# Three fp32r products for the scores of whole key chunks, and accumulating DMAs for a third of the softmax sums

## The chip, the cores and the metric

The kernel runs on one core of a Trainium2 chip. The metric is device time in microseconds (us): the median of separate runs of the whole program. One execution was also taken with the hardware profiler; all rows below come from it.

## What is computed

Soft-capped attention for 4 batches of 12 heads with 448 positions and 64 channels a head, and behind it a mixer over tokens and one over channels, each with a residual path. Cut to what matters:

```python
scores = scale * np.matmul(q, k.transpose(0, 1, 3, 2))
scores = cap * np.tanh(scores / cap)
attn = np.exp(scores - max)
attn = attn / (np.sum(attn, axis=-1, keepdims=True) + 1e-09)
x = np.matmul(attn, v)                     # heads side by side: 4 x 448 x 768
h = np.maximum(x^T @ w_tok1, 0.0) @ w_tok2
u = x + h^T
out = u + np.maximum(u @ w_ch1, 0.0) @ w_ch2
```

## The kernel before

Heads are worked in pairs: 24 pairs `(b, p)`, six a batch. A pair's queries and keys lie in one tile `qkraw` of 128 partitions, one head in partitions 0 to 63 and the other in 64 to 127, queries in `raw[:, 0]` and keys in `raw[:, 1]`. The 448 keys are cut into chunks: three whole ones of 128 and a rest of 64. A *unit* `(b, p, c)` is one chunk of a pair (`c` 0 to 2), or the rest of two neighbouring pairs packed together (`c == NF`), so that two pairs make seven units, and the kernel has 84.

For a unit TensorE forms the scores (`qk_unit`, L176), keys as weights and queries streamed, once for each head `j`, into two PSUM banks; a whole chunk takes two f32 matmuls at L182, one with the weights in the upper 64 rows of the array and one in the lower 64, and an f32 matmul runs as two instructions. ScalarE applies tanh into a tile `e` (L195; eight buffers for all units) and then exp in place (L200). TensorE multiplies by the values (L217, packed L226) and `evac` (L279, VectorE) empties that bank.

The sums over the keys that the softmax divides by are collected by `add_up` (L232). For chunk 1 VectorE adds chunks 0 and 1 into `acc` (L239), for chunk 2 it adds that chunk (L245), and `add_packed` adds the rest in two operations of 64 partitions (L257). An `e` buffer is free once its add is done. Two pairs share one `acc` tile; when both are done, `add_rows` (L259) sums over the partitions with matmuls against ones (L265), and `gather`, `norm`, `spread` and `scale_pair` follow one step apart: copies and small DMAs on SP's queue (`sums`, `rs`, `rb`), a reciprocal, and the multiply that writes `u` (L303). Only then can a pair be transposed (L326) for the token mixer.

Everything up to the end of the attention is in an order written out by hand: 42 steps of two units. In one step each engine gets, in this order, the multiplications by the values for the step's two units, the scores, tanh and exp of the units two steps ahead, the due evacuations, `add_up`, then `background` work, and last what was put off by `at(d, f, 2)` (`scale_pair` and the decoding of weights among it). `at(d, f, y)` runs `f` in place `y` of the step `d` later. `background` feeds TensorE with the token mixer of the batch before (L326, L353, L373), a budget of one ninth of a batch's work in every step. A tile's next load is issued once the last score that reads it has been issued: `load_pair` (L159) for the pair three further on, on SP's queue.

The weights come as 64-bit numbers and are decoded by VectorE, ScalarE and GpSimd (L99 to L119); GpSimd does one subtraction a piece (L119) and nothing else of weight. The token and channel mixers already use three products of high and low parts in fp32r (L353, L373, L552, L569); fp32r is a 4-byte type that TensorE multiplies in one instruction. The channel mixer begins at about 210 us and is not touched.

Of the kernel before, what the change touches and what calls it, by code (L numbers as in the profile page):

```python
# [9 lines left out]
F32R = mybir.dt.float32r  # L10
I32 = mybir.dt.int32
AF = mybir.ActivationFunctionType
ALU = mybir.AluOpType
PSUM = bass.MemoryType.PSUM

P = 128
B, H, S, D = 4, 12, 448, 64
# [6 lines left out]
NF = NK - 1  # L24
# [9 lines left out]
FREE = 40.0  # L34
EPS = 1e-9
WARM = 2


@with_exitstack
def tile_softcap_mixer(ctx, tc, qk, v, cap, w1, w2, wc1, wc2, out):  # L40
    nc = tc.nc
# [30 lines left out]
    def at(d, f, y=0):  # L72
        later.setdefault((now[0] + d, y), []).append(f)
# [76 lines left out]
    pi = in_att.enter_context(tc.tile_pool(name="pi", bufs=2))  # L150
# [3 lines left out]
    def half(i, j):  # L154
        return slice((i ^ j) * D, ((i ^ j) + 1) * D)

    raws = {}

    def load_pair(b, p):  # L159
        raw = pi.tile([P, 2, S], F32, tag="qkraw", name="qkraw", bufs=3)  # L160
        if b == 0 and p == 0:
            nc.sync.dma_start(raw[:, 0], qk[b, p, :, 0])
            nc.scalar.dma_start(raw[:, 1, :P], qk[b, p, :, 1, :P])
            nc.sync.dma_start(cap_sb, cap)
            nc.sync.dma_start(raw[:, 1, P:], qk[b, p, :, 1, P:])
        else:
            nc.sync.dma_start(raw, qk[b, p])
        raws[b, p] = raw

    def load_v(b, p):  # L170
        nc.sync.dma_start(vn[p % 3], v[b, p])

    scores = {}
    es = {}

    def qk_unit(b, p, c):  # L176
        ps = ps_a.tile([P, 2, 512], F32, tag="a", name="ps_qk")
        if c < NF:
            raw = raws[b, p]
            for j in range(2):  # L180
                r = slice(j * D, (j + 1) * D)
                nc.tensor.matmul(ps[:, j, :S], raw[r, 1, c * P:(c + 1) * P], raw[r, 0], start=True, stop=True)  # L182
        else:
            for i in range(2):
                raw = raws[b, p + i]
                for j in range(2):
                    r = slice(j * D, (j + 1) * D)
                    nc.tensor.matmul(  # L188
                        ps[half(i, j), i, :S], raw[r, 1, NF * P:S], raw[r, 0], start=True, stop=True
                    )  # L190
        scores[b, p, c] = ps
# [6 lines left out]
    def exp_unit(b, p, c):  # L198
        e = es[b, p, c]
        nc.scalar.activation(e, e, AF.Exp, scale=near)  # L200
# [29 lines left out]
    accs = {}  # L230

    def add_up(b, p, c):  # L232
        q, i = divmod(p, 2)
        if c == 0:
            return
        if c == 1:
            if i == 0:
                accs[b, q] = pe.tile([P, 2, 2, S], F32, tag="acc", name="acc", bufs=2)
            nc.vector.tensor_tensor(accs[b, q][:, i], es.pop((b, p, 0)), es.pop((b, p, 1)), op=ALU.add)  # L239
            if i == 1:  # L240
                add_packed(b, p)
                es.pop((b, p - 1, NF))
        elif c == 2:
            t = accs[b, q][:, i]
            nc.vector.tensor_tensor(t, t, es.pop((b, p, 2)), op=ALU.add)  # L245
            if i == 1:
                left[b] += 1
                at(1, lambda: work.insert(0, (add_rows(b, q), lambda: True)))
        else:
            add_packed(b, p)  # L250

    def add_packed(b, p):
        q, i = divmod(p, 2)
        for j in range(2):
            r = half(i, j)
            t = accs[b, q][r, i, j]
            nc.vector.tensor_tensor(t, t, es[b, p - i, NF][r, i], op=ALU.add)  # L257

    def add_rows(b, q):  # L259
        ps = ps_c.tile([P, 512], F32, tag="c", name="ps_s")  # L260
        acc = accs.pop((b, q))
        for i in range(2):
            for j in range(2):
                r = (2 * i + j) * SP
                nc.tensor.matmul(ps[r:r + SP, :S], ones, acc[:, i, j], start=True, stop=True, tile_position=(0, r))  # L265
        yield 750, True

        def take():
            x = px.tile([P, S], F32, tag="xs", name="xs", bufs=1)
            nc.vector.tensor_copy(x, ps[:, :S])  # L270
            at(pace[0], lambda: gather(b, q, x))

        read_at(b, None, take)
# [126 lines left out]
    work = []  # L400
# [56 lines left out]
    zeros = nc.const_aps.tensor(0.0, [P, HALF], F32)  # L457
    for _ in range(WARM):
        nc.tensor.matmul(idle[:, :HALF], zeros[:, :P], zeros, start=True, stop=True)
# [16 lines left out]
    def scores_of(t):  # L476
        two = units[2 * t:2 * t + 2]
        for unit in two:
            qk_unit(*unit)
        for unit in two:  # L480
            tanh_unit(*unit)
        for unit in two:
            exp_unit(*unit)
        for i in range(len(two)):
            for n, pair in enumerate(pairs):
                if last_score[pair] == 2 * t + i:
                    raws.pop(pair)
                    if n + 3 < len(pairs):
                        load_pair(*pairs[n + 3])

    scores_of(0)
    scores_of(1)
    for t in range(steps_in):
        two = units[2 * t:2 * t + 2]
# [10 lines left out]
        for b, p, c in two:  # L505
            add_up(b, p, c)
            n = pairs.index((b, p))
# [244 lines left out]
```

## Time and profile before

| | us |
|---|---|
| median of 3 runs | 606.57 (606.2 to 607.16) |
| the profiled execution | 605.01 |
| its span | 603.0 |
| TensorE busy in the span | 592.0 |
| VectorE busy | 384.9 |
| ScalarE busy | 254.5 |
| GpSimd busy | 54.5 |

The busy time is the union of an engine's instructions. A matmul's end is modelled, so that consecutive matmuls overlap in the records: the pace of a stream is read from its starts, or from a run of many. The chain of work that ended last follows the profile back from its end, at each step to what released the next piece. Times inside the program are counted from the span's start.

### The profile page before, as it was taken

How to read it: one execution, taken by the hardware profiler on the slowest of the kernel's cores; microseconds unless marked ns; L12 is line 12 of the kernel's file. 1: busy time of each engine (PE TensorE's matmuls, PEld its weight loads, DVE VectorE, ACT ScalarE, POOL GpSimd, SP SyncE). 2: the span in 40 equal slices, each digit the busy share in tenths (PEclk: the TensorE clock that was granted, in tenths of full speed). 3: DMA queues.
4: the chain of work that ended last, by engine and by line, in shares of the span. 5: the costliest groups of instructions: out<-in, count | busy, mean ns of one | idle time of the engine just before them, and what ended most of it. 6: DMA issues, size and time to landing. Idle time of an engine off the chain costs nothing.

```text
span 603.0 us, 7760 instructions
## 1 busy us (share of the span) xinstructions
PE 592.0 (98%) x3012; PEld 438.2 (73%) x3012; DVE 384.9 (64%) x626; ACT 254.5 (42%) x330; POOL 54.5 (9%) x48
## 2 busy tenths in 40 slices
PE   8998999999999999999999999999999999999997
PEld 2232444444444589997999999999989999999986
DVE  2899879696996996547788386438643853333324
ACT  7998987888878733114332122012211220000000
POOL 0021000000010000002331022001200120000000
PEclk9999999999999999999999999999999999999999
DMA  6545434244442201001343121202120200000224
GB/s 202 170 127 160 148 123 152 78 158 144 135 156 81 68 31 32 0 1 36 104 124 123 34 70 59 83 0 76 66 70 1 70 1 1 1 1 0 93 100 180
DMA packets 24620, 49.12 MB, mean 81 GB/s; under 512 B 6784, under 2 KB 16512, under 8 KB 24576
## 3 DMA queue, kind: packets, MB, share of 16 engines
q1 hardware_dynamic: 24288, 48.37, 24.9%
q8 instruction: 25, 0.41, 0.3%
q14 instruction: 19, 0.16, 0.1%
q10 hardware_dynamic: 288, 0.18, 0.1%
HBM read 42.86 MB, written 5.59 MB: 80 GB/s over the span
## 4 chain that ended last, share of the span: by engine, by line
PE 89%; DVE 5%; ACT 3%; issue 1%; DMA 1%; POOL 0%; SPq 0%; DVEq 0%
PE ps_g L552 29%; PE ps_o L569 29%; PE ps_pv L217 8%; PE ps_qk L182 8%; PE ps_h L353 5%; PE ps_u L373 5%; PE ps_s L265 2%; PE ps_pv L226 2%; PE ps_qk L188 1%; PE ps_t L326 1%; ACT e L195 1%; DVE acc L257 1%; ACT e L200 1%; DVE acc L239 1%; DMA qkraw<-in_qk 1%
## 5 line engine op out<-in xcount | busy, mean ns | idle before, releaser
L569 PE MATMUL ps_o<-g,wc 128*128 128x448 f32 x864 | 182.7, 367 | 0.0
L569 PEld LDWEIGHTS ps_o<-g,wc 128*128 128x128 f32 x864 | 161.6, 188 | 15.2 <-DVE u L574 0.9
L552 PE MATMUL ps_g<-uhl,wc 128*128 128x448 f32 x648 | 138.4, 367 | 0.0
L552 PEld LDWEIGHTS ps_g<-uhl,wc 128*128 128x128 f32 x648 | 120.9, 188 | 10.3
L574 DVE TENSOR_TENSOR u<-u,ps_o 128x448 f32<-128x448 f32 (+1 forms) x145 | 86.7, 612 | 46.8 <-PE ps_o L569 46.6
L195 ACT ACTIVATE e<-ps_qk,tsc 128x896 f32<-128x896 f32 x84 | 81.1, 1022 | 27.9 <-PE ps_qk L182 25.5
L200 ACT ACTIVATE e<-e,near 128x896 f32<-128x896 f32 x84 | 83.5, 1057 | 0.0
L119 POOL TENSOR_TENSOR wc<-wz,wc 128x512 fp32r<-128x512 f32 x36 | 48.2, 1341 | 385.4 <-ACT wc L118 361.9
L557 ACT ACTIVATE g<-ps_g 128x896 fp32r<-128x896 f32 x24 | 22.0, 916 | 142.5 <-PE ps_g L552 142.5
L558 DVE SCALAR_TENSOR_TENSOR g<-ps_g,g 128x896 fp32r<-128x896 f32 x24 | 26.1, 1088 | 75.1 <-ACT g L557 75.1
L182 PE MATMUL ps_qk<-qkraw 64*128 64x448 f32 x288 | 66.1, 570 | 1.0 <-DMA qkraw<-in_qk 0.9
L217 PE MATMUL ps_pv<-e,vn 128*64 128x448 f32 x288 | 64.2, 556 | 0.5 <-ACT e L195 0.5
L182 PEld LDWEIGHTS ps_qk<-qkraw 64*128 64x128 f32 x288 | 24.0, 186 | 42.9 <-issue 12.1
L118 ACT ACTIVATE wc<-wz 128x512 fp32r<-128x512 f32 x36 | 22.7, 629 | 74.6 <-PE ps_g L552 33.9
L552 PE MATMUL ps_g<-last_u,wc 128*128 128x448 f32 x216 | 45.6, 367 | 0.4 <-PE ps_o L569 0.3
L552 PEld LDWEIGHTS ps_g<-last_u,wc 128*128 128x128 f32 x216 | 40.4, 188 | 4.7 <-issue 0.7
L104 ACT ACTIVATE wz<-wraw 128x512 f32<-128x512 f32 x36 | 24.2, 673 | 46.1 <-DMA wraw<-in_wc 27.9
L217 PEld LDWEIGHTS ps_pv<-e,vn 128*64 128x64 f32 x288 | 16.5, 135 | 33.4 <-issue 15.9
L107 DVE TENSOR_SCALAR wz<-wz 128x512 f32<-128x512 f32 (+1 forms) x40 | 17.4, 435 | 34.8 <-ACT wz L104 34.7
L353 PEld LDWEIGHTS ps_h<-wc,last_u 128*128 128x128 f32 x176 | 30.4, 188 | 8.0 <-issue 6.0
L353 PE MATMUL ps_h<-wc,last_u 128*128 128x384 f32 x176 | 36.0, 343 | 0.0
L373 PE MATMUL ps_u<-last_u,wc 128*128 128x448 f32 x144 | 34.1, 375 | 1.5 <-DVE wc L362 0.8
(50 smaller groups left out, 414.3 us busy)
## 6 DMA issues: line engine op xcount, KB each, us to landing
wraw<-in_wc SPq DMA_DIRECT2D x36, 512.0 KB, 3.6
qkraw<-in_qk SPq DMA_DIRECT2D x23, 448.0 KB, 3.3
vn<-in_v SPq DMA_DIRECT2D x24, 224.0 KB, 3.4
rb<-rs SPq DMA_DIRECT2D x48, 112.0 KB, 2.8
out_t<-u SPq DMA_DIRECT2D x23, 224.0 KB, 1.9
wraw<-in_w SPq DMA_DIRECT2D x2, 512.0 KB, 4.7
wraw<-in_w SPq DMA_DIRECT2D x2, 448.0 KB, 3.7
sums<-xs SPq DMA_DIRECT2D x48, 1.8 KB, 2.3
```

The source lines that it names most:

```text
L104: nc.scalar.activation(zf, bits(r[:, :, 1]), AF.Abs, scale=2.0 ** -16)
L119: nc.gpsimd.tensor_tensor(lo, zf, hi, op=ALU.subtract)
L182: nc.tensor.matmul(ps[:, j, :S], raw[r, 1, c * P:(c + 1) * P], raw[r, 0], start=True, stop=True)
L195: nc.scalar.activation(e, scores.pop((b, p, c))[:, :, :S], AF.Tanh, scale=tsc)
L200: nc.scalar.activation(e, e, AF.Exp, scale=near)
L217: nc.tensor.matmul(ps[j * D:(j + 1) * D, :S], vn[p % 3][:, j * NF + c], es[b, p, c][:, j], start=first, stop=last)
L353: nc.tensor.matmul(ps[:, :HALF], w, x, start=(n == 0), stop=(n == len(mm) - 1))
L373: nc.tensor.matmul(ps[:, :S], h1[:, hi, t, cs], w2s[:, wi, t, :], start=(n == 0), stop=(n == 3 * NT - 1))
L552: nc.tensor.matmul(ps[:, i, :S], w[:, wi, cc, fs], uhl[b][:, ui, cc, :], start=(n == 0), stop=(n == 3 * NC - 1))
L558: nc.vector.scalar_tensor_tensor(g[:, 1], ps[:, :, :S], 0.0, g[:, 0], op0=ALU.max, op1=ALU.subtract)
L569: nc.tensor.matmul(ps[:, :S], w[:, wi, i, cs], g[:, gi, i, :], start=(n == 0), stop=(n == 3 * GF - 1))
L574: nc.vector.tensor_tensor(u[b][:, cc, r], u[b][:, cc, r], ps[:, r], op=ALU.add)
```

## The change

In batches 1 to 3 the scores of the whole chunks are formed from a high and a low part. For each pair there `load_pair` also issues, on GpSimd's queue, a DMA that reads the first 832 columns of the pair (448 of the queries, 384 of the keys) from memory a second time and casts them to fp32r (`hi`); two steps later VectorE subtracts it from `qkraw` into `lo`. `qk_unit` then issues three fp32r matmuls for each head (high by high, low by high, high by low) in place of one in f32, head by head within a term. The packed rest still reads `qkraw` in f32, and batch 0 is as before.

In batches 1 and 2 and in the first two thirds of batch 3 the add of chunk 2 (L245) is taken from VectorE: a DMA on GpSimd's queue adds the `e` tile into `acc`. For the first pair of two it is issued behind the packed add, one unit later than the add before; `add_rows` comes one step later. The region that GpSimd's DMA descriptors are kept in is cut to 4096 bytes a partition.

```diff
+SPLIT = S + NF * P
+TERMS = ((0, 0), (1, 0), (0, 1))
...
     def load_pair(b, p):
...
         raws[b, p] = raw
+        if b:
+            hi, lo = (pi.tile([P, SPLIT], F32R, tag=f"qk{x}", name=f"qk{x}", bufs=3) for x in ("hi", "lo"))
+            nc.gpsimd.dma_start(hi, qk[b, p].rearrange("p x s -> p (x s)")[:, :SPLIT])
+            rest = raw.rearrange("p x s -> p (x s)")[:, :SPLIT]
+            at(2, lambda: nc.vector.tensor_tensor(lo, rest, hi, op=ALU.subtract), 2)
+            parts[b, p] = hi, lo
...
     def qk_unit(b, p, c):
         ps = ps_a.tile([P, 2, 512], F32, tag="a", name="ps_qk")
-        if c < NF:
+        if c < NF and b:
+            two = parts[b, p]
+            ks = slice(S + c * P, S + (c + 1) * P)
+            for n, (x, y) in enumerate(TERMS):
+                for j in range(2):
+                    r = slice(j * D, (j + 1) * D)
+                    nc.tensor.matmul(ps[:, j, :S], two[x][r, ks], two[y][r, :S], start=(n == 0), stop=(n == 2))
+        elif c < NF:
...
     def add_up(b, p, c):
         q, i = divmod(p, 2)
+        by_dma = 0 < b < B - 1 or b == B - 1 and q < H // 4 - 1
...
         elif c == 2:
-            t = accs[b, q][:, i]
-            nc.vector.tensor_tensor(t, t, es.pop((b, p, 2)), op=ALU.add)
+            if not by_dma:
+                t = accs[b, q][:, i]
+                nc.vector.tensor_tensor(t, t, es.pop((b, p, 2)), op=ALU.add)
+            elif i == 1:
+                add_third(b, p)
             if i == 1:
                 left[b] += 1
-                at(1, lambda: work.insert(0, (add_rows(b, q), lambda: True)))
+                at(2 if by_dma else 1, lambda: work.insert(0, (add_rows(b, q), lambda: True)))
         else:
             add_packed(b, p)
+            if by_dma:
+                add_third(b, p)
+
+    def add_third(b, p):
+        q, i = divmod(p, 2)
+        nc.gpsimd.dma_start(accs[b, q][:, i], es.pop((b, p, 2)), accum_op=ALU.add)
...
-    nc = bacc.Bacc("TRN2", target_bir_lowering=False, num_devices=1)
+    nc = bacc.Bacc("TRN2", target_bir_lowering=False, num_devices=1, dynamic_dma_scratch_size=4096)
```

## Rows read from the trace of the kernel before

**Rows 1.** The page: engines' busy time, and TensorE's granted clock in 40 slices.

```profile
PE 592.0 (98%) x3012; PEld 438.2 (73%) x3012; DVE 384.9 (64%) x626; ACT 254.5 (42%) x330; POOL 54.5 (9%) x48
PEclk9999999999999999999999999999999999999999
```

**Rows 2.** Busy time by stretch: length, PE, PEld, DVE, ACT, POOL, clock, DMA, GB/s.

```profile
31.00:52.30 21.30, 19.01 (x104) 5.53 (x101) 20.76 (x33) 21.30 (x24) 3.88 (x4) 1.00 0.47 142
52.30:64.00 11.70, 11.67 (x68) 4.25 (x72) 11.48 (x20) 9.52 (x12) 1.13 (x1) 1.00 0.30 102
64.00:85.00 21.00, 21.00 (x122) 9.64 (x114) 16.78 (x28) 18.15 (x23) 0.00 (x0) 1.00 0.41 129
85.00:209.00 124.00, 122.13 (x664) 56.53 (x664) 101.43 (x167) 102.09 (x127) 7.98 (x6) 1.00 0.41 128
```

**Rows 3.** Waits of TensorE, 20 to 90 us: total us, times, longest.

```profile
PE ps_t L326 <- DVE u L303: 1.9, 1, 1.9
```

**Rows 4.** Longest wait of TensorE and of ScalarE, 64 to 209 us.

```profile
PE ps_t L326 <- DVE wc L340: 0.9, 2, 0.7
ACT e L195 <- PE ps_qk L182: 20.2, 14, 2.0
```

**Rows 5.** The chain that ended last, 30 to 82 us: start, us, what.

```profile
51.57 0.62 DVE u L303
...
52.33 1.10 PE ps_t L326 x8
...
66.96 1.70 PE ps_qk L182 x8
```

**Rows 6.** TensorE in order of time, two units' scores at 201 us: start, us.

```profile
201.13 0.65 PE L182 MATMUL ps_qk<-qkraw 64*128 64x448 f32 x2
...
201.99 0.92 PE L182 MATMUL ps_qk<-qkraw 64*128 64x448 f32 x4
202.37 0.54 PE L182 MATMUL ps_qk<-qkraw 64*128 64x448 f32 x2
202.84 0.47 PE L373 MATMUL ps_u<-last_u,wc 128*128 128x448 f32 x1
```

**Rows 7.** The chain that ended last, channel mixer: 36 fp32r matmuls.

```profile
296.84 7.36 PE ps_g L552 x36
```

**Rows 8.** VectorE's groups by shape up to 340 us: busy us, mean ns.

```profile
L245 DVE TENSOR_TENSOR acc<-acc,e 128x896 f32<-128x896 f32 x24 | 26.1, 1087 | 2.7 <-ACT e L200 2.0
L439 DVE TENSOR_TENSOR uhl<-u,uhl 128x448 fp32r<-128x448 f32 x18 | 10.4, 617 | 0.9 <-ACT uhl L438 0.6
L108 DVE TENSOR_SCALAR wz<-wz 128x512 int32<-128x512 int32 x22 | 10.8, 497 | 0.5
L108 DVE TENSOR_SCALAR wz<-wz 128x448 int32<-128x448 int32 x2 | 2.6, 1276 | 0.1
```

**Rows 9.** In order of time, single stretches of GpSimd, VectorE and ScalarE.

```profile
50.19 1.21 POOL L119 TENSOR_TENSOR last_u<-wz,last_u 128x448 fp32r<-128x448 f32 x1 [8.06 <-DVE last_u L116]
50.45 1.20 DVE L108 TENSOR_SCALAR wz<-wz 128x448 int32<-128x448 int32 x1
60.31 1.75 DVE L257 TENSOR_TENSOR acc<-acc,e 64x448 f32<-64x448 f32 x2
64.16 1.90 ACT L195 ACTIVATE e<-ps_qk,tsc 128x896 f32<-128x896 f32 x2
94.54 1.25 DVE L257 TENSOR_TENSOR acc<-acc,e 64x448 f32<-64x448 f32 x2
98.87 1.97 ACT L195 ACTIVATE e<-ps_qk,tsc 128x896 f32<-128x896 f32 x2 [1.60 <-PE ps_qk L182]
```

**Rows 10.** DMA issues: count, KB each, median us from issue to landing.

```profile
qkraw<-in_qk SPq DMA_DIRECT2D x23, 448.0 KB, 3.3
rb<-rs SPq DMA_DIRECT2D x48, 112.0 KB, 2.8
sums<-xs SPq DMA_DIRECT2D x48, 1.8 KB, 2.3
```

More of the change, by code (lines that the diff above doesn't have):

```diff
@@ L157, in tile_softcap_mixer @@
     raws = {}
+    parts = {}
     def load_pair(b, p):
@@ L487, in scores_of @@
                     raws.pop(pair)
+                    parts.pop(pair, None)
                     if n + 3 < len(pairs):
```

## The prediction

> **What bounds the kernel now.** I read the page first. TensorE is busy 98% of the span, at the upper of its two clock levels (2.4 GHz) in every slice [rows 1], so no time is to be had from the clock. An engine that full doesn't show where another sets the pace, so I read the busy times by stretch next. Up to about 52 us ScalarE is never idle (21.30 of 21.30) and VectorE nearly so (20.76), while TensorE has gaps; from 52.3 to 64 us VectorE is still full (11.48 of 11.70); from 64 us on TensorE is full and the other two have about a fifth of their time free [rows 2]. The waits say it more sharply. Before 64 us TensorE stands once for long, 1.9 us at a transpose that waits for VectorE's scaling [rows 3]; the chain that ended last runs over VectorE to that multiply and goes to TensorE with the transpose [rows 5]. From 64 to 209 us TensorE's longest wait is 0.9 us in all, and it is ScalarE that waits for TensorE's scores, 20.2 us [rows 4]. So a shorter score in batches 1 to 3 (they begin at about 45 us) is worth its full length from 64 us on, and work added to VectorE before 64 us is paid in full.
>
> **The scores: from 0.375 to 0.204 us a slot, but three slots for two.** Eight f32 instructions make two units. They start in twos, one for each half of the array's rows: 201.13, 201.99, 202.37 (with a start between the first two of these, left out), and the next work begins at 202.84 [rows 6]. So a unit is two slots of 0.375 us (202.37 less 201.99, rounded), and 1.71 - 4 x 0.375 = 0.21 us go to entering and leaving this tiling once for two units; that stays. After the change a unit is three slots of one fp32r pass. No row has such a pass with the array split. The nearest is the channel mixer's on the whole array, of the same 448 columns: 7.36 / 36 = 0.204 us [rows 7], weight load hidden. I take it. The gain is 54 units x (2 x 0.375 - 3 x 0.204) = 54 x 0.138 = 7.5 us. Bounds while the halves still run side by side: half an f32 slot, 0.1875 us, gives 10.1 us; a slot longer than the whole array's by a tenth, 0.224, for two weight loads and two banks at once, gives 4.2 us.
>
> **VectorE: 18 subtractions in, 16 adds out.** A subtraction has 832 elements a partition. Between 617 ns for 448 elements and 1087 ns for 896 [rows 8] that is 617 + 470 x 384 / 448 = 1020 ns, 18.4 us in all; the adds of chunk 2 that go are 16 x 1.087 = 17.4 us. In sum nothing, but not in place. The first pair of batch 1 is loaded in step 4, the next in steps 6, 8, 10 and 11, so that the subtractions stand in steps 6, 8, 10, 12 and 13. Two of them come before the scaling at 51.57 us, where VectorE is full, and the first add that goes is at step 11. VectorE's idle time in that stretch is 21.30 - 20.76 = 0.54 us [rows 2]. So the transpose at 52.33 us comes 2 x 1.02 - 0.54 = 1.5 us later, more if the idle bits can't be used: 1.8 us. Bounds: 0.5 (ScalarE, full as well, hides some) and 3.5 us (the third subtraction counts too, against one add). Behind 64 us VectorE has a fifth of its time to hide the rest.
>
> **GpSimd's queue: 18 casting and 16 accumulating DMAs.** The trace has no DMA of that queue. A casting load moves 416 KB and has two steps till its subtraction, at least eight of ScalarE's activations at 0.95 us each [rows 9], 7.6 us; loads of 448 KB on SP's queue land in 3.3 us [rows 10], so it costs nothing; if it were late, VectorE would stand, and with it everything of `add_up`. Queued on GpSimd behind a DMA that waits for VectorE are only later such DMAs and the decoding subtractions, whose results are needed from about 210 us on. The small DMAs of the softmax chain (2.3 and 2.8 us [rows 10]) have a step each, about 5 us from 64 us on (28 steps in 145 us).
>
> What an issue costs VectorE shows in two places: L108 takes 1.20 us, 497 ns elsewhere, while GpSimd works at 50.19 us, and the two adds at 60.31 us take 1.75 us where the same at 94.54 take 1.25 [rows 8, 9]. If each of the 34 issues holds VectorE up by 0.5 us, that is 17 us, nearly all in its free fifth; before 64 us it is some 5 issues. I put 0.5 us (0 to 2).
>
> **The accumulating DMA and the eight `e` buffers.** Before, chunk 2's buffer was free when VectorE had added it. Now, for the first pair of two, the DMA starts behind the packed add and the buffer is free when it has landed. Counting buffers through the steps: six belong to units ahead of `add_up`, and in one step of every seven two more are held by chunk 3 and by chunk 0 of the next pair, so that the second tanh of that step waits for this DMA. Four groups of pairs are concerned. In the first the packed adds end at 60.31 + 1.75 = 62.06 us and that tanh starts at 65.1 [rows 9]: 3.0 us. In the second it is 95.79 and 99.8: 4.0 us; the third and fourth, later still, I take to have as much or more. How long does the DMA take? Not under the 3.3 us of a load of that size; it also reads its destination, so half as much again, 5 us; the upper bound is three times a load, 10 us. At 5 us tanh is held 2.0 us in the first group; the score that needs the freed bank is the second unit of 66.96 [rows 5], at 67.8, and tanh ended at 66.06, so 1.7 us are covered and 0.3 us reach TensorE. In the second group 1.0 us is held, and the same cover is enough. At 10 us the first two groups give 5.3 and 4.3 us: 9.6. The sums' matmuls (L265) come one step later now, which is the 5 us.
>
> The Trainium skill has a fit for DMAs of this queue (DMA: Bandwidth & Descriptors, Anatomy of one DMA): 2.0 us and the bytes at 436 GB/s, an estimate of 3.1 us here, by which the 0.3 us would fall away. It says nothing of an accumulating one. Against this queue speaks SBUF — State Buffer, under two separate sides: while VectorE runs an operation in a two-port mode GpSimd cannot write descriptors. The trace shows the reverse side, VectorE held up beside GpSimd; no run here shows a DMA held up.
>
> **The sum.** Against the profiled execution: 605.01 - 7.5 + 1.8 + 0.5 + 0.3 = 600.1 us. The median of the runs is 1.56 us above it, so 601.7 us.
>
> **The rivals.** (a) *The halves don't run side by side in fp32r.* Every fp32r row of the trace uses the whole array, and every split one is f32, so nothing shows it. Then a unit is six slots: 54 x (6 x 0.204 - 0.75) = 25.6 us lost, with the costs 606.57 + 25.6 + 2.6 = 634.8 us. It decides from a slot of (0.75 - 2.6 / 54) / 3 = 0.234 us on. For overlap speaks that the f32 halves share the array through both passes [rows 6]. Chance 0.09. The Trainium skill (TensorEngine Tiling (Array Packing), Key Properties) says that tiles load weights and multiply in parallel, without a word on types; by it this rival falls.
> (b) *The accumulating DMA is slow.* At 10 us: 606.57 - 7.5 + 1.8 + 0.5 + 9.6 = 611.0 us. It decides where the two groups' waits make up the 5.2 us that are left of the gain, from a landing of about 7.8 us on. Chance 0.10.
> (c) *VectorE stays full beyond 64 us.* It gets GpSimd's hold-ups and five subtractions by step 13, and TensorE, now faster, waits for it at every transpose: 5 us in place of 2.3, with a slot of 0.21: 606.57 - 6.5 + 5 + 0.8 = 605.9 us. Against it stands its free fifth. Chance 0.11.
> (d) *More than the forecast.* Slots of 0.1875 us and only 0.5 us on VectorE: 606.57 - 10.1 + 0.5 = 597 us. Chance 0.07.
> The forecast has 0.63.
>
> **How the numbers follow.** A measurement of this kernel can tell 0.2% (1.2 us) from no change. The forecast's own bounds run from 598 to 605. The range takes in (b) and (c) and most of (d), 597.5 to 611, and leaves out (a) and the ends, under 0.2. Faster: the forecast and (d), 0.70; within 0.2%: (c), 0.11; slower: (a) and (b), 0.19.
>
> **What would show it.** Right: starts of the split fp32r matmuls 0.19 to 0.22 us apart in twos; a unit's scores at about 0.72 us; the first transpose wait (1.9 us before) at 3 to 4 us; ScalarE still waiting for TensorE behind 64 us; DMAs of `acc` landing in 4 to 7 us, with one short wait of tanh for them near 67 us. Wrong: starts one by one, 0.2 us apart (a); tanh waiting for `acc` DMAs in several groups (b); waits for VectorE spread over batches 1 and 2 (c).

## The result, and the profile after

The change makes the kernel slower: 611.48 us, median of 4 runs (610.84 to 611.83), against 606.38 us for the kernel before, measured beside it. The ratio is 1.0084, interval 1.0066 to 1.0102. The prediction was 601.7 us, 597.5 to 611, so it had the wrong sign, and the time lies just beyond its range. The profiled execution took 611.7 us with a span of 609.9 us, 6.9 us more than the span before (603.0).

The scores did what was forecast. In the chain that ended last (start, us, what) two units of scores take 1.42 us, where they took 1.70 before [rows 5]:

```profile
70.98 8.71 DMA acc<-e
...
83.78 1.42 PE ps_qk L193 x12
```

And in the order of time (start, us) the new matmuls start in twos, one for each half of the array's rows, 0.20 us apart (the first two of a step 0.31 us); the same view shows, 2 us later, a long stand:

```profile
45.57 0.47 PE L193 MATMUL ps_qk<-qkhi 64*128 64x448 f32 x2
45.88 0.36 PE L193 MATMUL ps_qk<-qkhi,qklo 64*128 64x448 f32 x2
...
46.08 0.36 PE L193 MATMUL ps_qk<-qklo,qkhi 64*128 64x448 f32 x2
46.28 0.37 PE L193 MATMUL ps_qk<-qkhi 64*128 64x448 f32 x2
...
49.53 1.02 DVE L176 TENSOR_TENSOR qklo<-qkraw,qkhi 128x832 fp32r<-128x832 f32 x1
...
50.46 0.62 DVE L305 COPY xr<-ps_pv 128x448 f32<-128x448 f32 x1
...
51.18 1.47 PE L233 MATMUL ps_pv<-e,vn 128*64 128x448 f32 x4 [3.22 <-ACT e L216]
...
55.14 1.15 DVE L329 TENSOR_TENSOR u<-xr,rb 128x448 f32<-128x448 f32 x2
```

So the 54 units win (1.70 - 1.42) / 2 = 0.14 us each, 7.6 us in all, and the change must cost about 7.6 + 6.9 = 14.5 us, where the prediction had 2.6. Where it goes shows in the page and in the busy times by stretch (columns as in [rows 2]):

```profile
PE 589.1 (97%) x3120; PEld 449.2 (74%) x3120; DVE 384.4 (63%) x628; ACT 255.1 (42%) x330; POOL 78.5 (13%) x82
PEclk8998999999999999999999999999999999999999
```

```profile
31.00:52.30 21.30, 18.08 (x106) 6.25 (x102) 20.32 (x32) 20.13 (x23) 4.39 (x5) 0.98 0.62 181
52.30:64.00 11.70, 10.36 (x68) 4.34 (x68) 11.52 (x21) 8.61 (x10) 3.05 (x4) 0.89 0.50 138
64.00:85.00 21.00, 18.34 (x117) 8.26 (x113) 16.39 (x25) 16.26 (x19) 4.07 (x6) 1.00 0.98 237
85.00:209.00 124.00, 118.50 (x748) 64.97 (x747) 96.27 (x163) 103.75 (x128) 25.83 (x30) 1.00 0.80 214
```

TensorE, which was full from 64 us on [rows 2], now has gaps in every stretch. VectorE has no more to do than before. New are the granted clock (under 1.00 in two slices of the page and in the first two stretches; it falls in some executions of the kernel before too, see the last section) and the DMA engines: their share goes from 0.41 to 0.98 and 0.80. The DMA issues (KB each, median us to landing) show what that does to the neighbours; the loads of keys took 3.3 us, the small `rb` and `sums` 2.8 and 2.3 [rows 10]:

```profile
qkraw<-in_qk SPq DMA_DIRECT2D x23, 448.0 KB, 5.1
qkhi<-in_qk POOLq DMA_DIRECT2D x18, 416.0 KB, 4.3
acc<-e POOLq DMA_DIRECT2D x16, 448.0 KB, 5.6
...
rb<-rs SPq DMA_DIRECT2D x48, 112.0 KB, 3.7
...
sums<-xs SPq DMA_DIRECT2D x48, 1.8 KB, 3.5
```

The waits from 64 to 209 us (total us, times, longest) name the followers. In [rows 4] TensorE's longest wait was 0.9 us in all, and before the change no engine waited for a DMA there for more than 0.3 us:

```profile
ACT e L211 <- PE ps_qk L193: 16.8, 14, 2.1
...
DVE sums L316 <- DMA sums<-xs: 6.0, 4, 2.6
...
ACT e L211 <- DMA acc<-e: 4.2, 4, 2.5
...
DVE u L329 <- DMA rb<-rs: 2.9, 2, 1.7
...
PE ps_t L352 <- DVE wc L366: 2.0, 3, 1.0
...
PE ps_qk L193 <- ACT e L211: 1.5, 2, 1.2
...
PE ps_s L291 <- DMA acc<-e: 1.1, 1, 1.1
```

The first group of accumulating DMAs shows how two of these waits come about (order of time):

```profile
66.04 0.91 POOL L276 DMA_DIRECT2D acc<-e  x1 [1.70 <-ACT e L211]
66.43 1.15 DVE L329 TENSOR_TENSOR u<-xr,rb 128x448 f32<-128x448 f32 x2
...
70.98 0.86 POOL L276 DMA_DIRECT2D acc<-e  x1 [2.51 <-DVE acc L283]
...
71.72 1.01 ACT L211 ACTIVATE e<-ps_qk,tsc 128x896 f32<-128x896 f32 x1 [2.47 <-DMA acc<-e]
...
72.78 0.47 PE L193 MATMUL ps_qk<-qkhi 64*128 64x448 f32 x2 [1.21 <-ACT e L211]
...
79.74 0.95 PE L291 MATMUL ps_s<-acc,ones 128*32 128x448 f32 x4 [1.06 <-DMA acc<-e]
```

The tanh at 71.72 us waits for the first of the two DMAs, which lands 5.6 us after its issue; the sums' matmul at 79.74 us waits for the second, which takes the 8.71 us shown above.

### The profile page after: what moved, and what is told of

It reads as the page before. It is cut to its first block, busy times and chain, and to the rows that moved or that the text cites. A ratio compares the mean times of both kernels' runs of the same rounds, so it can differ in the third digit from the quotient of the medians.

```text
span 609.9 us, 8104 instructions
## 1 busy us (share of the span) xinstructions
PE 589.1 (97%) x3120; PEld 449.2 (74%) x3120; DVE 384.4 (63%) x628; ACT 255.1 (42%) x330; POOL 78.5 (13%) x82
## 4 chain that ended last, share of the span: by engine, by line
PE 81%; DVE 8%; ACT 5%; issue 3%; DMA 3%; SPq 0%; POOL 0%; DVEq 0%; POOLq 0%; ACTq 0%
PE ps_g L579 29%; PE ps_o L596 29%; PE ps_pv L233 5%; PE ps_h L379 5%; PE ps_u L399 5%; PE ps_qk L193 3%; ACT e L216 2%; ACT e L211 2%; PE ps_qk L198 2%; DMA acc<-e 1%; DVE acc L283 1%; PE ps_qk L204 1%; PE ps_s L291 1%; PE ps_pv L242 1%; DVE acc L256 1%
## 5 line engine op out<-in xcount | busy, mean ns | idle before, releaser
L399 PEld LDWEIGHTS ps_u<-last_u,wc 128*128 128x128 f32 x144 | 25.7, 188 | 10.2 <-ACT e L211 2.7
L113 DVE SCALAR_TENSOR_TENSOR wz<-wraw,wz 128x512 int32<-128x512 int32 (+1 forms) x40 | 31.8, 796 | 0.7
```

The lines of the kernel that those rows point to most:

```text
L113: nc.vector.scalar_tensor_tensor(z, r[:, :, 1], -(1 << 31), z, op0=ALU.bitwise_and, op1=ALU.bitwise_or)
L399: nc.tensor.matmul(ps[:, :S], h1[:, hi, t, cs], w2s[:, wi, t, :], start=(n == 0), stop=(n == 3 * NT - 1))
```

## The experiments

For each kernel the tables below give the *lag*: how much later (us) the first multiplication by the values of one of the 42 steps starts than in the profile before, read from the order of time; "end" is the difference of the spans. In the profile before, step 12 begins at 58 us, step 16 at 75 us and step 41 at 208 us. A step with two split units should gain 0.28 us.

Where a kernel changes nothing between steps 10 and 12 and the lag still jumps by about 1.6 us (`x2_sums`, `y3_late`, `w3_free_late` and others), the granted clock fell there in its profiled execution, which it did not in the one before (last section).

Edits are shown against the changed kernel, cut to what matters. All of them keep the smaller region for DMA descriptors, which no run shows by itself; the lag of `y4_order` to step 12, 0.12 us, leaves little to it.

```
kernel                step 4  step 10  step 12  step 16  step 41    end
after                   1.23     0.79     4.24     6.77     5.08    6.9
x1_scores               2.51     1.78     5.85     4.87     3.64    4.5
x2_sums                -0.09    -0.09     1.54     0.69     3.39    5.0
x3_first_cast_late     -0.05    -0.49     3.26     5.41     3.68    5.3
y1_casts                1.52     1.52     1.68     1.68     1.71    2.6
y2_subs                -0.01    -0.02     2.52     2.52     3.95    4.9
y4_order                0.12     0.12     0.12    -0.74     1.57    3.1
y3_late                -0.64    -0.64     1.04     1.04     0.12    1.6
z1_free                -0.10    -0.54     1.30     0.30    -3.50    3.8
w3_free_late           -0.57    -0.58     1.01     1.01    -2.44   -1.0
z5_group               -0.13    -0.57     2.82     2.47    -0.90    0.1
y6_late_dma             0.27     0.28     0.27     0.28    -2.66   -0.6
z3_late_half           -0.14    -0.14     1.50     1.52     0.45    2.6
w1_from3               -0.72    -0.72     0.87     0.31    -3.04    2.9
w2_from3               -0.57    -0.57     1.10     0.54    -3.17    0.5
```

**Theory T** puts the loss on the transfers (casting loads, accumulating DMAs, the landings that they stretch); its rival, **theory V**, on VectorE (the subtractions, and what stands behind them). The first expectations call them A and B.

### One half of the change at a time

Split scores alone; all adds on VectorE.

```diff
-        by_dma = 0 < b < B - 1 or b == B - 1 and q < H // 4 - 1
+        by_dma = False
```

> The three-product scores with their casting loads and subtractions stay; the adds of chunk 2 go back to VectorE and the sums' matmuls to one step later, as before the change. Theory A (the accumulating DMAs fill the DMA engines, and their late landings are what eats the gain): the hold at the sums' matmul near 78 us (2.5 us) and the tanh waits for acc (4.2 us) go, 603 to 606 us. Theory B (VectorE is what eats the gain): 17 us of adds come back to VectorE, so no faster than the changed kernel, 611 us or more.

Measured: 609.25 us, ratio 1.0037 (1.0022 to 1.0052). Neither theory has that. It is 2.2 us late from step 5 on and loses 4.1 us at steps 11 and 12; from there to step 18 it wins 1.4 us, what six steps are due, and later it stands again. There it is VectorE: the sums' matmul waits for an eviction that stands behind a subtraction (order of time):

```profile
107.79 1.02 DVE L176 TENSOR_TENSOR qklo<-qkraw,qkhi 128x832 fp32r<-128x832 f32 x1
...
109.41 1.08 DVE L403 TENSOR_TENSOR u<-u,ps_u 128x448 f32<-128x448 f32 x2
...
110.02 0.96 PE L291 MATMUL ps_s<-acc,ones 128*32 128x448 f32 x8 [1.23 <-DVE u L403]
```

Accumulating DMAs alone; f32 scores, no casting load, no subtraction.

```diff
-        if b:
+        if False:
-        if c < NF and b:
+        if c < NF and False:
```

> Only the accumulating DMAs; scores in f32, no casting loads, no subtractions. Theory A: no gain from the scores and most of the loss, 609 to 613 us, with acc DMAs landing in 4 to 7 us, less than the 8.7 us beside casting loads. Theory B: VectorE has 17 us less to do and nothing else is touched, 604 to 606.4 us.

Measured: 609.56 us, ratio 1.0044 (1.003 to 1.0058), as theory T has it. So either half alone loses about 3 us, with landings of `acc` of 5.4 us in the median. That half takes away work from VectorE and still costs; `y4_order` below says why.

### The start

The first casting load two steps later, its subtraction one step later; the rest as changed.

```diff
-            nc.gpsimd.dma_start(hi, qk[b, p].rearrange("p x s -> p (x s)")[:, :SPLIT])
-            at(2, lambda: nc.vector.tensor_tensor(lo, rest, hi, op=ALU.subtract), 2)
+            load = lambda: nc.gpsimd.dma_start(hi, qk[b, p].rearrange("p x s -> p (x s)")[:, :SPLIT])
+            first = (b, p) == (1, 0)
+            at(2, load, 2) if first else load()
+            at(3 if first else 2, lambda: nc.vector.tensor_tensor(lo, rest, hi, op=ALU.subtract), 2)
```

> The changed kernel with one edit: the casting load of the first pair of batch 1, which waits for nothing and goes out at 1.5 us, is issued two steps later (behind GpSimd's first decoding subtraction, about 32 us), its subtraction one step later. If that load delays the program's first loads and TensorE's start: steps 4 to 10 run 1.2 us earlier again and the whole is 610.0 to 610.5 us. If the start's loss is made good anyway: 611.5 us, no change.

Measured: 610.07 us, ratio 1.005 (1.0036 to 1.0064). The lag at step 4 goes from 1.23 to -0.05 us and stays lower by 1.4 to the end. GpSimd's queue waits for nothing at the start, so the first casting load was issued at 1.5 us, among the first loads of queries and keys; in the changed kernel TensorE waits 1.8 us for one of these at 6.6 us, in the kernel before 0.9 us.

### Taking the split to GpSimd

High part by a copy on GpSimd, low part by a subtraction there; no new DMA, all adds on VectorE.

```diff
-            nc.gpsimd.dma_start(hi, qk[b, p].rearrange("p x s -> p (x s)")[:, :SPLIT])
-            at(2, lambda: nc.vector.tensor_tensor(lo, rest, hi, op=ALU.subtract), 2)
+            def split():
+                nc.gpsimd.tensor_copy(hi, rest)
+                nc.gpsimd.tensor_tensor(lo, rest, hi, op=ALU.subtract)
+            at(1, split, 2)
```

> Three-product scores, but no second load and no new DMA at all: GpSimd copies the high part out of the loaded pair and subtracts for the low part; adds of chunk 2 on VectorE. Theory A: no DMA is added, VectorE as before; the whole gain of 7.6 us less what GpSimd holds VectorE up, 599 to 602 us. Rival: GpSimd's 18 pairs of operations, about 1.2 and 2.2 us long, hold VectorE up for most of their length, 603 to 607 us.

Measured: 629.42 us, ratio 1.0379 (1.033 to 1.0428): both theories miss. VectorE has no more operations than in the kernel before, and they get longer. The groups by line (busy us, mean ns):

```profile
L287 DVE TENSOR_TENSOR acc<-acc,e 64x448 f32<-64x448 f32 x48 | 43.3, 903 | 1.2
L178 POOL TENSOR_TENSOR qklo<-qkraw,qkhi 128x832 fp32r<-128x832 f32 x18 | 40.1, 2228 | 1.4
...
L333 DVE TENSOR_TENSOR u<-xr,rb 128x448 f32<-128x448 f32 x24 | 24.5, 1053 | 1.8 <-DMA rb<-rs 1.7
```

The packed adds have a mean of 645 ns in the profile before and the scaling 658 ns; two scalings beside a copy and a subtraction on GpSimd take 3.48 us at 107.36. The Trainium skill (SBUF — State Buffer, Who interferes with whom) says that a VectorE instruction with two inputs in SBUF contends with a GpSimd instruction that reads SBUF; these rows agree. VectorE is then busy for 131.4 of the 145 us from 64 to 209 us, against 118.2 before, and TensorE's granted clock is 0.95 there in the mean; how much of the loss is the clock's isn't taken apart. This says nothing on theory V in the changed kernel.

### The loads and the subtractions, each by itself

Casting loads alone (f32 scores, no subtraction, adds on VectorE):

```diff
-            at(2, lambda: nc.vector.tensor_tensor(lo, rest, hi, op=ALU.subtract), 2)
-        if c < NF and b:
+        if c < NF and False:
-        by_dma = 0 < b < B - 1 or b == B - 1 and q < H // 4 - 1
+        by_dma = False
```

> The casting loads alone: scores stay f32, all adds on VectorE, no subtraction (the loaded high parts are read by nobody). Theory V, the loads' traffic costs only the start (1.2 us, as the kernel with the first of them later showed) and the rest of the loss is VectorE's: 607 to 608 us. Theory T, the traffic on the DMA engines also holds up the small transfers behind 64 us: 610 to 612 us.

Measured: 607.85 us, ratio 1.0022 (1.0002 to 1.0042). The lag is 1.52 us at step 4 and 1.71 at step 41: 18 casting loads of 416 KB cost TensorE 0.2 us apart from the start. Their traffic alone isn't the loss behind 64 us; theory T falls for the loads by themselves.

Subtractions alone (the rest as there):

```diff
-            nc.gpsimd.dma_start(hi, qk[b, p].rearrange("p x s -> p (x s)")[:, :SPLIT])
-            at(2, lambda: nc.vector.tensor_tensor(lo, rest, hi, op=ALU.subtract), 2)
+            at(2, lambda: nc.vector.tensor_tensor(lo, rest, rest, op=ALU.subtract), 2)
```

> The subtractions alone, where they stand in the changed kernel (low part = raw minus raw, read by nobody), f32 scores, no casting load, all adds on VectorE. Theory V: 2.3 to 3.6 us in the stretch before 64 us, where VectorE is full, and some 4 to 6 us behind it, where PSUM evictions stand behind a subtraction: 612 to 616 us. Theory T: only the first part, 608.5 to 610 us.

Measured: 610.05 us, ratio 1.0058 (1.0035 to 1.008): 2.5 us at steps 11 and 12 and 1.4 behind them, at the edge of theory T's range and under V's. The mechanism in the order of time:

```profile
47.81 1.02 DVE L175 TENSOR_TENSOR qklo<-qkraw 128x832 fp32r<-128x832 f32 x1
...
48.75 0.62 DVE L304 COPY xr<-ps_pv 128x448 f32<-128x448 f32 x1
...
49.47 0.97 PE L232 MATMUL ps_pv<-e,vn 128*64 128x448 f32 x4 [2.31 <-ACT e L215]
```

The eviction of a bank of value products (L304) stands behind the subtraction and starts 1.85 us later than in the kernel before (46.90 us there): 1.0 us by this subtraction, 0.9 by the first one, which VectorE hasn't made up. So the bank is free later, and TensorE waits 2.31 us for it; the profile names ScalarE, which had long been done (in the profile before, the wait there was 0.45 us, at 47.62). This is the stand of the changed kernel at 51.18 us, above. The wait at the transpose stays at 1.9 us, as in [rows 3].

### The order by itself

The kernel before, with the sums' matmuls one step later in the eight groups (the expectation miscounts them) that the change takes to DMAs; no DMA added.

```diff
-        if b:
+        if False:
-        if c < NF and b:
+        if c < NF and False:
-        by_dma = 0 < b < B - 1 or b == B - 1 and q < H // 4 - 1
+        by_dma = False
-                at(2 if by_dma else 1, lambda: work.insert(0, (add_rows(b, q), lambda: True)))
+                at(2 if 0 < b < B - 1 or b == B - 1 and q < H // 4 - 1 else 1, lambda: work.insert(0, (add_rows(b, q), lambda: True)))
```

> The kernel before with one thing moved: the sums' matmuls of the seven groups one step later, as the changed kernel has them; no DMA is added, f32 scores, all adds on VectorE. If the 3.2 us that the accumulating DMAs cost alone are their landings and traffic: 606 to 607 us. If the later place of the sums in the softmax chain is the cost: 608 to 609.5 us.

Measured: 608.96 us, ratio 1.0029 (1.0009 to 1.005). So the later place is most of what `x2_sums` lost (ratio 1.0044): from step 16 on the two kernels' lags move together, -0.74 to 1.57 and 0.69 to 3.39; the 1.4 to 1.8 us between them are there from step 12 on, with the clock's fall in the profile of `x2_sums`. The softmax chain (sums, reciprocal, broadcast, scaling, transpose) starts later by a step, and the rest of the side work moves with it.

### The gain with nothing added

Three fp32r products from one fixed high part, in batches 1 to 3 (`z1_free`) and in batches 2 and 3 (`w3_free_late`); the scores are not the right ones, and all adds are on VectorE.

```diff
-        if b:
-            hi, lo = (pi.tile([P, SPLIT], F32R, tag=f"qk{x}", name=f"qk{x}", bufs=3) for x in ("hi", "lo"))
+        if (b, p) == (0, 1):
+            one = pi.tile([P, SPLIT], F32R, tag="qkhi", name="qkhi", bufs=1)
...
+            at(2, lambda: nc.gpsimd.tensor_copy(one, rest), 2)
+            fixed.append(one)
...
-            two = parts[b, p]
+            two = fixed * 2
...
-        by_dma = 0 < b < B - 1 or b == B - 1 and q < H // 4 - 1
+        by_dma = False
```

> The scores' shorter time on TensorE with nothing added: in batches 1 to 3 the three fp32r products of every unit are made from one fixed high part, rounded once by GpSimd in batch 0 (so these scores are not the right ones), with no casting load and no subtraction; all adds on VectorE. If the gain is worth its full length, 54 x 0.14 = 7.6 us: 598 to 600 us. If something else comes due at every step as TensorE gets faster, half of it is lost with nothing added: 601.5 to 604 us.

Measured: 608.21 us, ratio 1.003 (1.0013 to 1.0048): beyond both answers. To step 41 it goes as "half of it is lost" has it: from step 16 to 41 the lag falls by 3.8 us, where about 5.7 are due; TensorE's longest waits there are for VectorE's copies of transposes (L352 behind L366, 1.8 us, where the kernel before has 0.9; L291 behind it, 1.1, before 0.4). Then 7.3 us are lost behind step 41. The largest piece is one stand in the last stage (TensorE's waits from 560 to 590 us, and the busy times of the two stretches):

```profile
PE ps_g L579 <- issue: 4.0, 1, 4.0
```

```profile
571.80:581.80 10.00, 6.00 (x26) 5.33 (x25) 2.49 (x5) 0.00 (x0) 0.00 (x0) 0.88 0.40 147
581.80:586.80 5.00, 5.00 (x24) 4.58 (x24) 0.00 (x0) 0.00 (x0) 0.00 (x0) 0.90 0.00 0
```

TensorE waits for nothing that the profile shows, and after the stand its granted clock is at the lower level for a while.

> The scores' shorter time on TensorE in batches 2 and 3 alone, with nothing added (three fp32r products from one fixed high part, so these scores are not the right ones; no casting load, no subtraction, all adds on VectorE). The like in batches 1 to 3 had won 3.5 us by the end of batch 3 and then lost 4.0 us at one place of the last stage, where TensorE stood at the first score of the channel mixer's last group with no releaser, plus 3 us in small pieces. If that stand belongs to the place where instructions are fetched, it depends on the length of TensorE's program, which is shorter here: the stand differs from 4.0 us, and the time is 602 to 604.5 us. If it belongs to TensorE being ahead there: 4 us again, 605 to 607 us.

Measured: 603.41 us, ratio 0.9949 (0.9932 to 0.9965). The stand is 1.3 us here, 1.1 in the changed kernel, 0.3 in the one before. Of 36 x 0.14 = 5.0 us this kernel keeps 3.1 by the ratio. Three of its four runs have the granted clock 0.997; against the runs of the kernel before at 0.997 they are 3.8 us faster. So even for nothing, a shorter score is worth about two thirds to three quarters of its length here, not all of it.

### Where to split

Batches 2 and 3 alone, adds on VectorE; then the same with accumulating DMAs for the first pair of every two, the sums in their old step; then with all of the DMAs and the later sums, as changed.

```diff
-        if b:
+        if b > 1:
-        if c < NF and b:
+        if c < NF and b > 1:
-        by_dma = 0 < b < B - 1 or b == B - 1 and q < H // 4 - 1
+        by_dma = False                                              # y3_late
+        by_dma = i == 0 and b > 1                                   # z3_late_half
+        by_dma = 1 < b < B - 1 or b == B - 1 and q < H // 4 - 1     # y6_late_dma
-                at(2 if by_dma else 1, lambda: work.insert(0, (add_rows(b, q), lambda: True)))
+                at(1, lambda: work.insert(0, (add_rows(b, q), lambda: True)))     # z3_late_half
```

> Split scores in batches 2 and 3 alone, with their casting loads and subtractions (batch 1 stays f32), all adds on VectorE. Gain 36 units x 0.14 = 5.0 us. If the scores' cost falls nearly all before 85 us (start 1.2, stretch before 64 us 2.4 to 3.6): 601.5 to 603 us, faster than both. If it falls behind 85 us in proportion to the units: 604.5 to 606.5 us.

> Split scores in batches 2 and 3 alone, as in the kernel that measured 0.9998; here, in the same batches, the first pair of every two has its third chunk added by an accumulating DMA (it has a step to land), the second pair on VectorE, and the sums' matmuls stay in their old step. VectorE theory (what ate the gain there were PSUM evictions behind the subtractions): half of the load is taken from it, 603 to 605 us. Transfer theory (accumulating DMAs cost by their landings and traffic): 606.5 to 609 us.

> Split scores and accumulating DMAs, as the changed kernel has them, in batches 2 and 3 alone; batch 1 as before. The start, the stretch before 64 us and the collision at 70 us are left out. If these three make up the whole loss of the changed kernel (6 to 7 us of it): 602 to 604 us. If the later place of the sums' matmuls costs again what it cost alone (1.5 us) and the landings as much: 605.5 to 608 us.

Measured: 606.66 us, ratio 0.9998 (0.9973 to 1.0023); 606.28 us, 0.9991 (0.9978 to 1.0005); 604.98 us, 0.9965 (0.9944 to 0.9986). The first, just above its second answer, gives the 5.0 us of gain back whole, though it leaves the steps before 85 us as they were. The second lies between its theories' answers and settles nothing. The third, between its two answers, beats its neighbours: with subtractions on VectorE and scores shorter, taking all the third-chunk adds away is worth more than the later sums cost. In batches 2 and 3 the two halves of the change seem to help each other; no run has the accumulating DMAs of these batches alone.

The changed kernel with the start mended and the first group of batch 1 left on VectorE:

```diff
-        by_dma = 0 < b < B - 1 or b == B - 1 and q < H // 4 - 1
+        by_dma = (b, q) != (1, 0) and 0 < b < B - 1 or b == B - 1 and q < H // 4 - 1
```

> The changed kernel with the first casting load two steps later (610.1 us alone) and the first group of batch 1 with its sums on VectorE and in their old step, so that no accumulating DMA is among the transfers at 68 to 80 us. If the collision of five transfers there is what costs the 2.5 us of step 16: 607 to 608 us. If VectorE, which gets two adds back in a stretch where it has little room, loses as much: 609.5 to 611 us.

Measured: 605.42 us, ratio 0.9985 (0.9972 to 0.9997), 4.65 us under `x3_first_cast_late` by the times and 3.9 by the two ratios, a larger gain than either answer. One group of the eight costs more than the 2.9 us by which that kernel stood above the one before: with the start and this group mended, the change is no longer slower. The busy times from 68 to 82 us (columns as before), first of `x3_first_cast_late`, then of `z5_group`, then of `x2_sums`, which has that group's DMAs but no casting loads:

```profile
68.00:82.00 14.00, 11.72 (x69) 4.89 (x67) 10.41 (x17) 11.47 (x14) 2.30 (x3) 1.00 1.02 243
```

```profile
68.00:82.00 14.00, 14.00 (x91) 7.99 (x92) 12.50 (x19) 12.98 (x16) 1.96 (x3) 1.00 0.77 210
```

```profile
68.00:82.00 14.00, 14.00 (x77) 6.53 (x75) 8.73 (x14) 13.12 (x16) 1.72 (x2) 1.00 0.88 209
```

With that group's two DMAs the DMA engines are full (1.02) and TensorE stands 2.3 us; without them it stands not at all, though VectorE does 2.1 us more. Nor does it in `x2_sums`, where the two land in 5.0 and 6.4 us; but there the scores are in f32 and the subtractions gone as well. So the two DMAs alone don't make the stand. That the full DMA engines do is argued from their share: no run leaves out one of the other transfers. In the changed kernel five transfers are issued close together there (casting load 67.92, queries and keys 68.56, weights 68.94, values 69.80, accumulating DMA 70.98 us), and the last lands after 8.71 us.

Split from the fourth pair of batch 1 on, with accumulating DMAs from its second or its third group on:

```diff
-        if b:
+        if (b, p) >= (1, 3):
-        if c < NF and b:
+        if c < NF and (b, p) >= (1, 3):
-        by_dma = 0 < b < B - 1 or b == B - 1 and q < H // 4 - 1
+        by_dma = (b, q) >= (1, 1) and b < B - 1 or b == B - 1 and q < H // 4 - 1     # w1_from3
+        by_dma = (b, q) >= (1, 2) and b < B - 1 or b == B - 1 and q < H // 4 - 1     # w2_from3
```

> The changed kernel with split scores from the fourth pair of batch 1 on and accumulating DMAs from the second group of batch 1 on; before that everything as in the kernel before. No casting load in the first steps, no subtraction before 58 us, no accumulating DMA among the transfers of 68 to 80 us. Against the kernel with batches 2 and 3 alone (0.9965): 9 more units, 1.3 us, and two more groups by DMA. If these only cost by the three places left out: 603 to 604.5 us. If each group's later sums and landings cost again (0.5 us a group and more): 605 to 606.5 us.

> As the kernel beside it, but accumulating DMAs only from the third group of batch 1 on. If VectorE's room between 64 and 85 us counts more than the landings: slower than its neighbour by 0.5 to 1.5 us. If the landings count more: faster by as much.

Measured: 606.10 us, ratio 0.9987 (0.9971 to 1.0003), and 604.64 us, ratio 0.9967 (0.995 to 0.9984). By the times the landings count more, as the last answer has it; by the lags not: at step 41 the two are level (-3.04 and -3.17); the first loses its advantage behind it (stands of 2.2 and 0.9 us at the last group of the channel mixer, 1.7 and 0.9 in the second), so that the group by DMA isn't shown to be worse. The second is, with `y6_late_dma`, the best kernel of the study that has the right scores, 0.33% under the one before (`y6_late_dma` 0.35%).

## Why the prediction was wrong, point by point

Three steps failed. The accumulating DMA was priced at 0.3 us of TensorE, and its first group alone costs 3.9 to 4.65 us. The sums' matmuls one step later were priced at nothing, and cost 1.8 us by themselves. VectorE's subtractions were priced at 1.8 us, and that stretch before 64 us costs 3.9 us (2.5 with the subtractions alone). With them a premise failed, that a shorter score is worth its full length behind 64 us.

**What bounds the kernel: half right.** "A shorter score is worth its full length from 64 us on" is the premise that reaches furthest. TensorE was full there, and its longest wait was 0.9 us, but the profile of before can't show how near the next thing is. `w3_free_late` shows it: with nothing added 3.1 to 3.8 of 5.0 us remain. As TensorE gets ahead, its waits for VectorE's copies of the transposes grow from 0.9 to 1.8 us.

**Scores: right.** A slot of 0.20 us (0.204 forecast), 0.14 us a unit (0.138), 7.6 us (7.5). Rival (a) falls on the starts in twos.

**VectorE, 1.8 us with bounds of 0.5 to 3.5: under-sized, and by another road.** The forecast looked at the scaling and the transpose. What is late first is the eviction of a bank of value products, 3 us earlier, which stands in the same queue behind the subtraction; `y2_subs` has 2.5 us for it before 64 us and 1.4 behind. In the changed kernel the lag grows by 3.45 us from step 10 to 12, where 0.4 us more of gain were due: 3.9 us. The 1.4 us beyond `y2_subs` aren't the granted clock's, though it falls after the stand (0.57 from 51 to 55 us). VectorE begins that subtraction 1.7 us later than in `y2_subs` (49.53 against 47.81 us), some 1.2 of it from the start, and the scaling as much later (55.14 against 53.42). TensorE, brought forward to a lag of 0.79 us by its first shorter scores, only waits longer for the same bank. The slow clock falls into the wait at the transpose, which is 0.45 us there, where 3 to 4 were forecast and 1.9 stood before.

**"So it costs nothing" (casting loads): wrong at one place.** Behind the start it holds (0.2 us, `y1_casts`). At the start nothing holds GpSimd's queue back, and the load meets the first key loads: 1.2 to 1.5 us (`x3_first_cast_late`, `y1_casts`; 2.2 in `x1_scores`). Beside accumulating DMAs it isn't shown: the casting load of 67.92 us is among the transfers of the collision. The order in which the queue runs was considered for what it is moved past, not for how early it can run.

**The accumulating DMA, 5 us and 0.3 us of TensorE: the landing right, the price wrong.** The DMA that the second tanh of the step waits for lands in 5.6 us in the first group (66.04 to 71.64). That tanh is held 2.5 us, forecast 2.0; of the cover of 1.7 us only 1.3 was there, so the score waits 1.2 us. In the other three groups concerned tanh is held 0.8, 0.7 and 0.3 us and no score waits. This mechanism was right, and small. What the sum has no term for is the second pair's DMA, behind which the sums' matmul stands: beside the four other transfers it lands in 8.71 us, and TensorE waits 1.1 us for it. The prediction took the landing of one DMA with little beside it, while the change adds 15.0 MB on GpSimd's queue. In all the first group costs 3.9 to 4.65 us (`x3_first_cast_late` against `z5_group`).

**"The sums' matmuls come one step later now, which is the 5 us": priced at nothing, costs by itself.** `y4_order` has a ratio of 1.0029 for it, 1.8 us. The small DMAs with "a step each" belong here: `sums` and `rb` land 1.2 and 0.9 us later, and VectorE stands 8.9 us for them between 64 and 209 us.

**GpSimd's hold-ups, 0.5 us: not there.** The two places that the term was read from stand beside GpSimd's decoding subtractions (50.19 and, not in [rows 9], 59.81 us), not beside an issue. In the changed kernel the packed adds that run beside an issue take 614 ns in the mean (five of them), and forty others 619; the two scalings beside the issue at 66.04 us take 1.15 us, as those at 51.57 us in the kernel before. One packed add beside a subtraction takes 1133 ns.

**The sum, from the lags.** Gain -7.6; start 1.3; before 64 us 3.9; steps 13 to 16, 4.24 to 6.77 where a fall of 1.0 was due, 3.5; steps 17 to 41, 6.77 to 5.08 where a fall of about 5.7 was due, 4.0, of which about 1.9 are lost in `z1_free` with nothing added; behind step 41 1.8, of which 0.8 are the longer stand at the channel mixer's last group. Together 6.9 us; measured 6.9. These pieces say when the time is lost; that the start and the first group are enough to turn the sign is shown by the runs without them, `x3_first_cast_late` and `z5_group`.

**The rivals.** The time, 611.5, is that of (b), 611.0, but by luck: (b) put 9.6 us on tanh's waits in two groups, with landings of 10 us, where tanh waits 4.2 us in four groups, with landings of 4.2 to 5.6 us, and TensorE sees 1.2 us of it. (c), whose sum counts GpSimd's 0.5 us twice, has VectorE full beyond 64 us, and that is what `x1_scores` shows; in the changed kernel the accumulating DMAs take that load away, and put the order and the landings in its place.

**What stays open.** Why TensorE stands, with no releaser, at the first matmul of the channel mixer's last group (0.3 us before, up to 1.2 in most kernels, 1.3 to 4.0 in four; in `z1_free` and `w1_from3` the granted clock fell behind it), and why the kernels that were most ahead at step 41 (-3.50, -3.17, -3.04) lost most behind it (7.3, 3.7, 5.9 us), was not settled. `w3_free_late` has the time and the stand of its first answer, a shorter program, but it was also less ahead, so that the second isn't excluded.

## What to carry to other kernels

Before a saving on a full engine is booked at its full length, find how late the next engine already is, by a kernel that saves the time and adds nothing. Price a moved step by itself, even if it moves by one step only, and look in each queue past which work is moved for the first thing that stands behind it, such as an eviction that frees a bank. A DMA's landing depends on what runs beside it: list what else is in flight at each new transfer, above all at the start, where a queue with nothing to wait for runs ahead.

## What the runs showed of the hardware that was not expected

- Three fp32r matmuls with the array split in two halves of 64 rows start in pairs 0.20 us apart at 448 columns, as fast as one on the whole array (0.204 us [rows 7]). The Trainium skill (TensorEngine Tiling (Array Packing), Key Properties) has no word on types; here its rule holds for fp32r.
- GpSimd's copy and subtraction of 832 elements take 1.19 and 2.23 us, and VectorE's two-input operations take up to 1.6 times as long in the mean in that kernel (658 to 1053 ns). Beside GpSimd's issues of DMAs the same operations take no longer (614 against 619 ns for a packed add in the changed kernel).
- A casting load of 416 KB lands in 4.3 us, an accumulating DMA of 448 KB in 5.4 to 6.3 us in the median (`x2_sums`, `y6_late_dma`), against 3.3 us for a plain load of that size in the kernel before; at a DMA share of about 1.0 it took 8.7 us.
- The granted clock falls to its lower level (1.2 of 2.4 GHz) for about 3.5 us (7 in `z5_group`) in or behind the stands of TensorE between 46 and 57 us, in some runs of a kernel and not in others. In `x2_sums`, as in the kernel before, these stands are 0.4 and 1.9 us, and the fall comes at 53.4 us. The kernel before, measured with the first four experiments, took 606.15 us in the mean of 10 runs whose mean granted clock was 1.0, and 607.87 us in 11 runs at 0.997: runs with the fall are 1.7 us longer. The stretch from 52 to 58 us shows it, first in the profile of `y4_order`, which has none, then in that of `x2_sums`:

```profile
52.00:58.00 6.00, 5.55 (x34) 2.37 (x36) 5.89 (x12) 4.45 (x6) 0.00 (x0) 1.00 0.32 111
```

```profile
52.00:58.00 6.00, 5.77 (x24) 2.40 (x24) 5.89 (x12) 2.81 (x5) 0.00 (x0) 0.72 0.27 81
```

TensorE is nearly as busy in both and gets through 34 and 24 matmuls.
